# Loading q and k of two heads with one transfer, and taking the second batch's first unit by float32 rows

## Chip, core and metric

The kernel runs on one core of a Trainium2 chip. The metric is the device time of one execution in microseconds, the median of several runs. The engines are PE (TensorE, matmuls), ACT (ScalarE), DVE (VectorE), POOL (GpSimd) and SP (SyncE, which issues all transfers here).

## What is computed

Causal attention with a decay on 4 batches x 8 heads of 576 positions (head dimension 64), and then two feed-forward layers on the 2304 rows that come out of it:

```python
scores = scale * np.matmul(q, k.transpose(0, 1, 3, 2))
log_f = np.log(np.clip(f, 0.0001, 1.0))
cum = np.cumsum(log_f, axis=-1)
scores = np.where(causal, -1000000000.0, scores + cum[..., :, None] - cum[..., None, :])
attn = np.exp(scores - max);  attn = attn / (sum + 1e-09);  x = attn @ v
h = x @ w_in;   y = np.maximum(0.01 * h, h) @ w_out                 # 512 -> 2048 -> 512
g = y @ w_gate; out = (g * sigmoid(g) * (y @ w_val)) @ w_out2       # 512 -> 1536 -> 512
```

All results are float32.

## The kernel before

The program is recorded as a list of operations and put in order by a planner (`Plan`), which knows what each operation reads and writes, estimates durations, and writes out one fixed order for each of the five engines. Each engine, and SP's queue of transfers too, then works through its own order; a transfer on SP whose data isn't ready holds up all that stand behind it. In the first microseconds the planner fills pauses of PE with matmuls that nobody uses.

Attention goes by units: unit (b, u) is batch b, queries 0 to 319 (u = 0, three tiles of queries a head) or 320 to 575 (u = 1, two tiles). Unit (0,0) has a path of its own; the other seven go through `attention`. While a unit's attention runs, PE does the first feed-forward layers (`moe_h`, then `moe_y`) of the unit before; the weights of the second feed-forward layers are loaded, converted and written back in the same time (`place`, from unit (1,1) on). After unit (3,1), at about 500 us, only feed-forward work is left.

For each head `prep_head` loads q and k and `exps` makes the scores, by one of two ways:

- In batch 0, "float32 rows": a tile of 66 rows, 64 of q and k and two that carry the cumulative sums (`rd`), and one plain float32 matmul for each part of a query tile.
- In batches 1 to 3: the host stores q and k twice below each other, so that one transfer of 128 rows (640 columns for u = 0, 832 for u = 1) puts the same 64 rows on both halves of the partitions. ACT casts all 128 rows to a reduced float32 (tile `ta`) and casts the q part to `tb`; DVE subtracts what the cast lost, q into the upper half of `ta` and k into the lower half of `tb`. Four rows of cumulative sums go to `tb` by a transfer of their own. A score part is then two matmuls, one from `tb` (68 rows) and one from `ta` (128 rows). The loads go to two buffers (`xf_ring`), a head each.

The scores go through DVE (mask, maximum), ACT (exponential), and ACT and DVE (probabilities as two float16 parts). A DMA transpose turns them; when both heads of a pair are there, `pv` multiplies them with v on PE, one group of 24 (u = 0) or 30 (u = 1) matmuls with 64 columns of weights, which alternate between the two heads.

Buffers: the g buffers of the feed-forward layer (`g_ring`) are separate for u = 0 and u = 1, 20,480 and 16,384 bytes a partition. The latter's bytes are used under the name `early` until the end of unit (0,1), among others for three more tiles of 66 rows (`xf1_ring`).

Of the kernel before, what the change touches and what calls it, by code (L numbers as in the profile page):

```python
# [9 lines left out]
F32 = mybir.dt.float32  # L10
F32R = mybir.dt.float32r
F16 = mybir.dt.float16
# [9 lines left out]
P = 128  # L22
# [425 lines left out]
def body(ctx, tc, qk, v, f, w_in, w_out, w_gate, w_val, w_out2, out):  # L448
# [38 lines left out]
    gvd = tc.dram_tile([2 * NB2, P, NC * FB2], F32, name="gate_val_dram")  # L487
    cd = tc.dram_tile([R, 4, W], F32, name="cum_dram")
    rd = tc.dram_tile([H, 2, KEYS[1] + UNITS[1][1]], F32, name="rows_dram")


    pool = ctx.enter_context(tc.tile_pool(name="sb", bufs=1))
# [14 lines left out]
    wo_f = wo_t.t.rearrange("p (a d) -> p a d", d=DM)  # L507
    wo = wo_t.t.bitcast(F16).rearrange("p (a l d) -> p a l d", l=2, d=DM)
    PER = [512 // u[1] for u in UNITS]
    g_ring = [Ring([x.rearrange("p (l i q) -> p l i q", l=2, i=n) for x in a_g.cut(2 * n * u[1], F16, NF // n).bufs])  # L510
              for n, u in zip(PER, UNITS)]
    xs_buf = [a_m.cut(NC * 2 * u[1], F16).rearrange("p (c l q) -> p c l q", c=NC, l=2) for u in UNITS]
    n = a_m.at
    gf_ring = [None, None]
# [20 lines left out]
    vv_ring = Ring([x.rearrange("p (c j l d) -> p c j l d", j=2, l=2, d=D) for x in a_a.cut(NK * 4 * D, F16, 5).bufs])  # L535


    early = a_g.t[:, (a_g.at - NF * 2 * UNITS[1][1] * 2) // 4:]
    dg_ring = Ring([early[:, (i + 1) * P:(i + 2) * P] for i in range(3)])
    vf0 = [early[:, 4 * P + i * NK * P:4 * P + (i + 1) * NK * P].rearrange("p (c d) -> p c d", d=P) for i in range(NHP)]  # L540
    n = 4 * P
# [83 lines left out]
    def decay():  # L625
        n0 = UNITS[0][1]
        scr = wo_t.t[:R, :]
        fr, cum, one = (scr[:, i * S:(i + 1) * S] for i in range(3))
        nc.vector.memset(one[:, :S - n0], -8.0)
        one = one[:, S - n0:]  # L630
        nc.urgent = True
        nc.sync.dma_start(fr, f)
        nc.vector.memset(one, 1.0)
        nc.vector.tensor_scalar(out=fr, in0=fr, scalar1=1e-4, scalar2=1.0, op0=ALU.max, op1=ALU.min)
        nc.scalar.activation(out=fr, in_=fr, func=AF.Ln)

        nc.scalar.activation(out=sm(1, "e", 1)[:R, :], in_=fr[:, :1], func=AF.Exp)

        nc.vector.memset(rows0[:, :n0], 8.0)
        nc.vector.memset(rows0[:, 2 * n0:], -8.0)  # L640
        c0 = rows0[:, n0:2 * n0]
        nc.vector.tensor_tensor_scan(out=c0, data0=one, data1=fr[:, :n0], initial=0.0, op0=ALU.mult, op1=ALU.add)

        lib = sm(1, "lib", 1)
        nc.gpsimd.memset(lib, 0.0)
        nc.gpsimd.partition_all_reduce(lib, lib, P, ABSMAX)
        nc.gpsimd.memset(mask, 0.0)
        nc.urgent = False
        scan = next(o for o in reversed(nc.ops) if o.eng == "DVE")

        nc.filler = (banks[-1], mask[:, :P], mask[:, :4 * P])
        nc.gpsimd.affine_select(out=mask[:, 4 * P:], in_=mask[:, 4 * P:], pattern=[[-1, P + hw]],
                                compare_op=ALU.is_ge, fill=NEG, base=0, channel_multiplier=1)
        csf = scr[:, 3 * S:3 * S + 4 * W].rearrange("r (a s) -> r a s", a=4)
        cs = csf.bitcast(F32R)

        for x in ph_ring.bufs:
            for i in (3, 8):
                nc.gpsimd.memset(x.rearrange("p (n k) -> p n k", k=P)[:, i::9, hw:], 0.0)
        nc.behind = scan  # L660
        for u, (q0, nq, _) in enumerate(UNITS):
            col, _, qc, kc = COLS[u]
            for a, c, n in ((0, kc, KEYS[u]), (2, qc, nq)):
                x = csf[:, a:a + 2, col + c:col + c + n]
                nc.scalar.copy(out=x, in_=one[:, :1].unsqueeze(2).to_broadcast(x.shape))
        nc.behind = None
        nc.scalar.copy(out=cum[:, :n0], in_=c0)
        nc.vector.tensor_tensor_scan(out=cum[:, n0:], data0=one[:, :S - n0], data1=fr[:, n0:],
                                     initial=c0[:, n0 - 1:n0], op0=ALU.mult, op1=ALU.add)
        nc.vector.memset(fr, 8.0)  # L670
        for u, (q0, nq, _) in enumerate(UNITS):
            col, wd, qc, kc = COLS[u]
            n = KEYS[u]
            ks = slice(col + kc, col + kc + n)
            qs = slice(col + qc, col + qc + nq)
            nc.vector.tensor_scalar(out=cs[:, 2, ks], in0=cum[:, :n], scalar1=-8.0, scalar2=None, op0=ALU.mult)
            nc.vector.scalar_tensor_tensor(out=cs[:, 3, ks], in0=cum[:, :n], scalar=-8.0, in1=csf[:, 2, ks],
                                           op0=ALU.mult, op1=ALU.subtract)
            nc.scalar.activation(out=cs[:, 0, qs], in_=cum[:, q0:q0 + nq], func=AF.Copy, scale=8.0)
            nc.scalar.activation(out=cs[:, 1, qs], in_=csf[:, 3, col + kc + q0:col + kc + n], func=AF.Copy, scale=-1.0)  # L680
        nc.sync.dma_start(cd, csf)
        nc.sync.dma_start(rd[:, 0, :S], fr[:H, :])
        nc.sync.dma_start(rd[:, 0, S:], cum[:H, n0:])
        nc.sync.dma_start(rd[:, 1, :], scr[:H, S:3 * S - n0])
# [4 lines left out]
    def prep_v(b, hps):  # L689
# [19 lines left out]
        if hp == NHP - 1:  # L709
# [5 lines left out]
            nc.vector.tensor_scalar(out=sc, in0=iv, scalar1=sx, scalar2=1.0 / PSCALE, op0=ALU.mult, op1=ALU.mult)  # L715
            vsc[b] = (sc, ix, sx)

    class Head:
        pass

    def prep_head(b, u, h):
        o = Head()
        o.b, o.u, o.tp, o.sums = b, u, [], sm(3, "sums", 4)
        nq, nk = UNITS[u][1], KEYS[u]
        col, o.wd, qc, kc = COLS[u]
        o.q, o.k = slice(qc, qc + nq), slice(kc, kc + nk)
        if b == 0:
            o.xf = xf1_ring.next()
            nc.sync.dma_start(o.xf[:D, :o.wd], qk[b, h, :D, col:col + o.wd])
            nc.sync.dma_start(o.xf[D:D + 2, :o.wd], rd[h])  # L730
            return o
        xf = xf_ring.next()
        nc.sync.dma_start(xf[:, :o.wd], qk[b, h, :, col:col + o.wd])
        o.tb = tb_ring.next()
        nc.sync.dma_start(o.tb[D:D + 4, :o.wd].bitcast(F32), cd[b * H + h, :, col:col + o.wd])
        o.ta = ta_ring.next()
        taf = o.ta.bitcast(F32)
        nc.scalar.copy(out=o.ta[:, :o.wd], in_=xf[:, :o.wd])
        nc.scalar.copy(out=o.tb[:D, o.q], in_=taf[:D, o.q])
        nc.vector.tensor_tensor(out=o.ta[D:, o.q], in0=xf[D:, o.q], in1=taf[D:, o.q], op=ALU.subtract)  # L740
        nc.vector.tensor_tensor(out=o.tb[:D, o.k], in0=xf[:D, o.k], in1=taf[:D, o.k], op=ALU.subtract)
        return o

    def exp_of(tp, parts, ms, mx, total):
# [12 lines left out]
    def exps(o, n):  # L757
# [10 lines left out]
        nc.begin()  # L768
        for a, e, w in parts:
            ps = ps_s.next()  # L770
            if o.b == 0:
                nc.tensor.matmul(ps[:, :w], lhsT=o.xf[:D + 2, q:q + P],
                                 rhs=o.xf[:D + 2, o.k.start + a:o.k.start + a + w], start=True, stop=True)
            for l in range(2 if o.b else 0):
                t, k = (o.tb, D + 4) if l == 0 else (o.ta, P)
                nc.tensor.matmul(ps[:, :w], lhsT=t[:k, q:q + P], rhs=t[:k, o.k.start + a:o.k.start + a + w],
                                 start=(l == 0), stop=(l == 1))
# [343 lines left out]

    for arena in (a_a, a_g, a_m, wi_t, wo_t, a_w):
        arena.at = 0
    WB = NB2 * 2
    NW = [WB - 4, 2, 2]
    w2 = [x.rearrange("p (k l d) -> p k l d", k=14, l=2)
          for t, n in zip((a_a, a_g, wi_t), NW) for x in t.cut(14 * 2 * P, F16, n).bufs]
# [6 lines left out]
    c_ring = Ring([x.rearrange("p (m k n) -> p m k n", m=2, k=4) for x in wi_t.cut(8 * UH, F32, 2).bufs])  # L1134
    waste2 = wi_t.cut(UN, BF16, 2)

    us_0 = [x.rearrange("p (l a n) -> p l a n", l=2, a=NA)
            for t, n in ((a_g, 6), (a_a, 1)) for x in t.cut(2 * NA * P, F16, n).bufs]
    sum_t = a_g.cut(NA * P, F32).rearrange("p (a n) -> p a n", a=NA)
# [328 lines left out]
```

## Time and profile before

| | us |
|---|---|
| median of 3 runs | 923.5 (923.33 to 925.16) |
| the profiled execution | 925.66 |
| its span, first to last instruction | 923.9 |
| PE busy | 908.8 (98%) |
| DVE busy | 794.1 (86%) |
| ACT busy | 676.1 (73%) |
| POOL busy | 45.4 (5%) |
| DMA engines, mean busy share | 54.2% |

Busy times are unions of an engine's instructions, and ends of matmuls are modelled, so PE's busy share is not a share of its peak. A plain float32 matmul shows as two records, all others as one. What a matmul costs PE is read from the distance between starts. The kernel has a heavy attention part up to about 500 us, in which all engines and the DMA queues are loaded, and a part of matmuls alone after it.

### The profile page before, as it was taken

How to read it: one execution, taken by the hardware profiler on the slowest of the kernel's cores; microseconds unless marked ns; L12 is line 12 of the kernel's file. 1: busy time of each engine (PE TensorE's matmuls, PEld its weight loads, DVE VectorE, ACT ScalarE, POOL GpSimd, SP SyncE). 2: the span in 40 equal slices, each digit the busy share in tenths (PEclk: the TensorE clock that was granted, in tenths of full speed). 3: DMA queues.
4: the chain of work that ended last, by engine and by line, in shares of the span. 5: the costliest groups of instructions: out<-in, count | busy, mean ns of one | idle time of the engine just before them, and what ended most of it. 6: DMA issues, size and time to landing. Idle time of an engine off the chain costs nothing.

```text
span 923.9 us, 25387 instructions
## 1 busy us (share of the span) xinstructions
PE 908.8 (98%) x10018; PEld 776.7 (84%) x10018; DVE 794.1 (86%) x2078; ACT 676.1 (73%) x1665; POOL 45.4 (5%) x119
## 2 busy tenths in 40 slices
PE   9999999999999999899999999999999999999998
PEld 5666678877688777788778899999999999999997
DVE  7999999988899999799788999986778695968685
ACT  8886689988689887688886878774647474755553
POOL 3410000000000010000000000000000000000000
PEclk9999999999999999999999999999999999999999
DMA  7568985797999999989867452110101000100001
GB/s 229 179 202 217 271 212 115 187 248 172 259 270 259 255 263 229 298 249 254 188 147 191 140 178 96 64 59 20 37 18 31 25 25 25 37 25 2 26 6 42
DMA packets 163431, 132.81 MB, mean 144 GB/s; under 512 B 117432, under 2 KB 130752, under 8 KB 163280
## 3 DMA queue, kind: packets, MB, share of 16 engines
q1 hardware_dynamic: 163312, 131.20, 53.5%
q8 instruction: 78, 1.28, 0.6%
q14 instruction: 41, 0.34, 0.1%
HBM read 79.99 MB, written 22.83 MB: 111 GB/s over the span
## 4 chain that ended last, share of the span: by engine, by line
PE 58%; DVE 7%; DMA 3%; ACT 3%; issue 1%; POOL 0%; SPq 0%; ACTq 0%; DVEq 0%; POOLq 0%
PE bank L415 58%; DVE att_bytes L415 2%; DVE stage L415 1%; DVE wo_bytes L415 1%; ACT att_bytes L415 1%; DMA tb<-out_dram 1%; ACT moe_bytes L415 1%; DMA att_bytes<-att_bytes 1%; DVE smalls L415 1%; DVE wi_bytes L415 1%; DMA att_bytes<-in_qk_dram 1%; DMA gate_val_dram<-wo_bytes 1%; DVE g_bytes L415 1%; DVE tb L415 0%; DVE ta L415 0%
## 5 line engine op out<-in xcount | busy, mean ns | idle before, releaser
L415 PEld LDWEIGHTS <-att_bytes 128*128 128x128 f16 (+1 forms) x4062 | 233.8, 100 | 18.3 <-issue 14.7
L415 PEld LDWEIGHTS <-wi_bytes 128*128 128x128 f16 x2292 | 192.2, 98 | 42.4 <-issue 3.1
L415 PE MATMUL bank<-g_bytes,wo_bytes 128*128 128x256 f16 (+2 forms) x1472 | 209.7, 299 | 0.0
L415 PE MATMUL bank<-moe_bytes,wi_bytes 128*128 128x320 f16 (+1 forms) x1536 | 194.5, 286 | 1.5 <-ACT moe_bytes L415 1.5
L415 ACT ACTIVATE att_bytes<-att_bytes,smalls 128x320 f32<-128x320 f32 (+11 forms) x308 | 173.7, 591 | 30.1 <-DVE smalls L415 25.5
L415 PEld LDWEIGHTS <-wo_bytes 128*128 128x128 f16 x1344 | 128.1, 98 | 33.5 <-issue 1.8
L415 DVE TENSOR_TENSOR wi_bytes<-bank,wi_bytes 128x256 f32<-128x256 f32 x270 | 109.4, 418 | 45.0 <-PE bank L415 43.6
L415 PEld LDWEIGHTS <-g_bytes 128*128 128x128 f16 x1620 | 125.9, 98 | 9.0
L415 ACT ACTIVATE wi_bytes<-wi_bytes,smalls 128x256 f32<-128x256 f32 (+2 forms) x129 | 69.9, 555 | 44.9 <-DVE wi_bytes L415 42.4
L415 PE MATMUL bank<-wi_bytes,att_bytes 128*128 128x128 f16 x1680 | 98.7, 219 | 0.5 <-ACT wi_bytes L415 0.3
L415 DVE SCALAR_TENSOR_TENSOR att_bytes<-att_bytes,smalls 128x576 f16<-128x576 f32 (+5 forms) x148 | 86.8, 614 | 4.1 <-ACT att_bytes L415 3.7
L415 PE MATMUL bank<-stage,att_bytes 128*128 128x128 f16 (+1 forms) x1389 | 86.7, 221 | 0.6 <-DVE wi_bytes L415 0.6
L415 ACT COPY wi_bytes<-bank 128x256 f32<-128x256 f32 x108 | 38.4, 363 | 51.8 <-PE bank L415 47.6
L415 DVE CUSTOM_DVE_ANT_0 att_bytes<-bank,att_bytes 128x320 f32<-128x320 f32 (+5 forms) x160 | 67.7, 441 | 7.2 <-PE bank L415 7.1
L415 POOL PARTITION_ALL_REDUCE smalls<-smalls x54 | 28.2, 523 | 757.1 <-DVE smalls L415 718.3
L415 PE MATMUL bank<-att_bytes 128*64 128x256 f16 (+4 forms) x828 | 55.5, 262 | 5.5 <-DMA att_bytes<-att_bytes 5.2
L415 ACT ACTIVATE wi_bytes<-wo_bytes 128x256 bf16<-128x256 f32 x108 | 44.0, 410 | 19.2 <-DVE wo_bytes L415 19.2
L415 PE MATMUL bank<-wo_bytes,g_bytes 128*128 128x256 f16 x432 | 55.0, 273 | 0.0
L415 DVE TENSOR_TENSOR g_bytes<-moe_bytes,g_bytes 128x320 f16<-128x320 f32 (+1 forms) x80 | 44.6, 564 | 8.2 <-ACT g_bytes L415 7.8
L415 PE MATMUL bank<-tb 68*128 68x256 f32 (+3 forms) x144 | 49.9, 360 | 1.7 <-ACT att_bytes L415 1.1
L415 DVE SCALAR_TENSOR_TENSOR stage<-stage 128x512 int32<-128x512 int32 x68 | 46.5, 684 | 0.2
L415 DVE SCALAR_TENSOR_TENSOR wo_bytes<-wi_bytes,smalls 128x512 f32<-128x512 f32 x54 | 40.1, 743 | 6.3 <-ACT wi_bytes L415 6.3
(123 smaller groups left out, 1380.1 us busy)
## 6 DMA issues: line engine op xcount, KB each, us to landing
stage<-in_moe_w_out_dram SPq DMA_DIRECT2D x28, 512.0 KB
att_bytes<-in_qk_dram SPq DMA_DIRECT2D x24, 416.0 KB
stage<-in_moe_w_in_dram SPq DMA_DIRECT2D x16, 512.0 KB
att_bytes<-in_qk_dram SPq DMA_DIRECT2D x24, 320.0 KB
stage<-in_moe_w_gate_dram SPq DMA_DIRECT2D x12, 512.0 KB
stage<-in_moe_w_val_dram SPq DMA_DIRECT2D x12, 512.0 KB
stage<-gate_val_dram SPq DMA_DIRECT2D x12, 512.0 KB
ta<-y_dram SPq DMA_DIRECT2D x18, 256.0 KB
```

What stands on the lines that cost most here:

```text
L415: fn(*args, **kw)
```

## The change

1. In batches 1 to 3 one transfer of 128 rows serves two heads: it begins at the second copy of the even head and ends with the first copy of the odd one, so that the even head lies on the lower and the odd head on the upper half of the partitions. Each head is then prepared from its own half. The cast to `ta` becomes two, of 64 partitions each: all columns to the lower half, and the k columns (320 or 576) to the upper half, which the 128-row cast covered before.
2. Unit (1,0) goes by float32 rows as batch 0 does, with five tiles in `xf1_ring`; its rows come from a new small DRAM tensor (`rd0`) that is written once.
3. Both units' g buffers begin at the same byte, and `early`, which is now in use until the end of unit (1,0), lies behind them. Two weight tiles of the last part move to the end of the same memory.

```diff
+    rd0 = tc.dram_tile([H, 3 * UNITS[0][1]], F32, name="rows0_dram")
...
+    g_ring = []
+    for n, u in zip(PER, UNITS):
+        a_g.at = 0
+        x = a_g.cut(2 * n * u[1], F16, NF // n).bufs
+        g_ring.append(Ring([y.rearrange("p (l i q) -> p l i q", l=2, i=n) for y in x]))
...
-    early = a_g.t[:, (a_g.at - NF * 2 * UNITS[1][1] * 2) // 4:]
+    early = a_g.t[:, NF * UNITS[0][1]:]
...
+        nc.sync.dma_start(rd0, rows0[H:2 * H, :])
...
-        if b == 0:
+        o.one = b + u == 1
+        if o.one:
             o.xf = xf1_ring.next()
             nc.sync.dma_start(o.xf[:D, :o.wd], qk[b, h, :D, col:col + o.wd])
-            nc.sync.dma_start(o.xf[D:D + 2, :o.wd], rd[h])
+            r = rd0[h]
+            nc.sync.dma_start(o.xf[D:D + 2, :o.wd], rd[h] if u else bass.AP(r.tensor, r.offset, [[nq, 2], [1, o.wd]]))
             return o
-        xf = xf_ring.next()
-        nc.sync.dma_start(xf[:, :o.wd], qk[b, h, :, col:col + o.wd])
+        x = h % 2
+        if x == 0:
+            both[0] = xf_ring.next()
+            a = qk[b, h, D:, col:col + o.wd]
+            nc.sync.dma_start(both[0][:, :o.wd], bass.AP(a.tensor, a.offset, [[a.ap[0][0], P], a.ap[1]]))
+        xf = both[0][x * D:(x + 1) * D]
...
-        nc.scalar.copy(out=o.ta[:, :o.wd], in_=xf[:, :o.wd])
+        nc.scalar.copy(out=o.ta[:D, :o.wd], in_=xf[:, :o.wd])
+        nc.scalar.copy(out=o.ta[D:, o.k], in_=xf[:, o.k])
         nc.scalar.copy(out=o.tb[:D, o.q], in_=taf[:D, o.q])
-        nc.vector.tensor_tensor(out=o.ta[D:, o.q], in0=xf[D:, o.q], in1=taf[D:, o.q], op=ALU.subtract)
-        nc.vector.tensor_tensor(out=o.tb[:D, o.k], in0=xf[:D, o.k], in1=taf[:D, o.k], op=ALU.subtract)
+        nc.vector.tensor_tensor(out=o.ta[D:, o.q], in0=xf[:, o.q], in1=taf[:D, o.q], op=ALU.subtract)
+        nc.vector.tensor_tensor(out=o.tb[:D, o.k], in0=xf[:, o.k], in1=taf[:D, o.k], op=ALU.subtract)
...
-            if o.b == 0:
+            if o.one:
...
+    a_g.at = a_g.size - 2 * 14 * 2 * P * 2
```

The planner makes a new order of everything. In it PE's matmuls that nobody uses go from 44 to 43. At three places it reads as follows. On PE, at the first head of unit (1,0), before (`tb` and `ta` are the prepared tiles, `g_bytes,wo_bytes` is feed-forward work of unit (0,0)):

```order
L415 MATMUL bank_69<-tb_86 128x256
L415 MATMUL bank_69<-ta_84 128x256
L415 MATMUL bank_70<-tb_86 128x256
L415 MATMUL bank_70<-ta_84 128x256
L415 MATMUL bank_73<-g_bytes,wo_bytes 128x320
```

and now (tiles of 66 rows lie in `g_bytes` and `att_bytes`):

```order
L415 MATMUL bank_71<-g_bytes 128x256
L415 MATMUL bank_70<-g_bytes 128x256
L415 MATMUL bank_72<-g_bytes 128x320
L415 MATMUL bank_75<-g_bytes,wo_bytes 128x320
L415 MATMUL bank_76<-g_bytes,wo_bytes 128x320
L415 MATMUL bank_71<-g_bytes 128x256
L415 MATMUL bank_70<-g_bytes 128x256
L415 MATMUL bank_72<-g_bytes 128x320
```

Three matmuls a head take the place of six, and the second head's stand close behind the first's.

On SP, at the end of unit (2,1), from the third last transpose of its probabilities to the last, before (`in_qk_dram` is a q/k load, `tb` a transfer of cumulative sums):

```order
L415 DMA_TRANSPOSE att_bytes<-att_bytes 128x18x128
L415 DMA tb_87<-cum_dram 4x640
L415 DMA att_bytes<-in_v_dram 128x640
L415 DMA_TRANSPOSE att_bytes<-att_bytes 128x18x128
L415 DMA stage<-in_moe_w_out_dram 128x1024
L415 DMA att_bytes<-in_qk_dram 128x640
L415 DMA out_dram<-wi_bytes 128x512
L415 DMA att_bytes<-in_qk_dram 128x640
L415 DMA_TRANSPOSE att_bytes<-att_bytes 128x18x128
```

and now:

```order
L415 DMA_TRANSPOSE att_bytes<-att_bytes 128x18x128
L415 DMA out_dram<-wi_bytes 128x512
L415 DMA tb_87<-cum_dram 4x640
L415 DMA att_bytes<-in_qk_dram 128x640
L415 DMA_TRANSPOSE att_bytes<-att_bytes 128x18x128
L415 DMA tb_88<-cum_dram 4x640
L415 DMA stage<-in_moe_w_out_dram 128x1024
L415 DMA_TRANSPOSE att_bytes<-att_bytes 128x18x128
```

Four transfers stood before the last transpose, two of them q/k loads; now two do, and neither is a q/k load. One stands before the transpose ahead of it.

On ACT, at the first heads of unit (1,1), now (`ta` and `tb` casts of two heads; before, each pair of `ta` casts was one of 128x832):

```order
L415 CAST ta_85<-att_bytes 64x832
L415 CAST ta_85<-att_bytes 64x576
L415 CAST tb_87<-ta_85 64x256
L415 ACTIVATE moe_bytes<-bank_73,smalls 128x320
L415 CAST ta_86<-att_bytes 64x832
L415 CAST ta_86<-att_bytes 64x576
L415 CAST tb_88<-ta_86 64x256
```

Each head has one cast more, right behind the first.

## Rows read from the trace of the kernel before

**Rows 1.** The page's busy times: us, share of the span, instructions.

```profile
PE 908.8 (98%) x10018; PEld 776.7 (84%) x10018; DVE 794.1 (86%) x2078; ACT 676.1 (73%) x1665; POOL 45.4 (5%) x119
```

**Rows 2.** Windows of about units (1,0), (2,0) and (3,0); columns in the first line.

```profile
core 0: us, PE busy (x) PEld busy (x) DVE busy (x) ACT busy (x) POOL busy (x), PEclk, DMA share, GB/s
112.00:185.00 73.00, 71.88 (x644) 60.59 (x641) 69.35 (x208) 67.28 (x167) 3.65 (x12) 1.00 0.76 176
252.00:307.00 55.00, 53.91 (x531) 46.80 (x532) 51.92 (x171) 49.12 (x131) 3.69 (x11) 1.00 0.97 257
376.00:433.00 57.00, 57.00 (x549) 49.54 (x547) 52.64 (x162) 49.02 (x130) 0.30 (x2) 0.97 0.95 260
```

**Rows 3.** PE's waits: who for whom, us in total, times, longest.

```profile
PE bank L415 <- DMA att_bytes<-att_bytes: 5.2, 3, 2.3
...
PE bank L415 <- ACT moe_bytes L415: 1.5, 3, 0.7
PE bank L415 <- ACT att_bytes L415: 1.1, 1, 1.1
```

**Rows 4.** Timeline of PE at 371: start, us, instruction, idle before it.

```profile
371.05 0.39 PE L415 MATMUL bank<-tb 68*128 68x256 f32 x1
...
372.03 0.30 PE L415 MATMUL bank<-att_bytes 128*64 128x256 f16 x1
374.68 0.52 PE L415 MATMUL bank<-att_bytes 128*64 128x256 f16 x6 [2.35 <-DMA att_bytes<-att_bytes]
```

**Rows 5.** Timeline of PE at 96: matmuls of 66 rows in unit (0,1).

```profile
96.02 1.14 PE L415 MATMUL bank<-g_bytes 66*128 66x288 f32 x4
97.00 0.70 PE L415 MATMUL bank<-g_bytes,wo_bytes 128*128 128x320 f32 x2
97.54 0.92 PE L415 MATMUL bank<-g_bytes 66*128 66x448 f32 x2
98.29 0.43 PE L415 MATMUL bank<-g_bytes,wo_bytes 128*128 128x320 f32 x1
```

**Rows 6.** Timeline of PE at its other waits in the attention part.

```profile
110.64 1.56 PE L415 MATMUL bank<-att_bytes 128*64 128x256 f16 x29 [1.26 <-DMA att_bytes<-att_bytes]
...
172.36 0.39 PE L415 MATMUL bank<-tb 68*128 68x320 f32 x1 [1.12 <-ACT att_bytes L415]
...
252.31 1.56 PE L415 MATMUL bank<-att_bytes 128*64 128x256 f16 x29 [1.62 <-DMA att_bytes<-att_bytes]
...
435.75 0.43 PE L415 MATMUL bank<-moe_bytes,wi_bytes 128*128 128x320 f16 x2 [0.71 <-ACT moe_bytes L415]
```

**Rows 7.** Timeline of SP ahead of the longest of these waits.

```profile
365.61 0.53 SPq L415 DMA_DIRECT2D stage<-in_moe_w_out_dram  x1
366.19 0.42 SPq L415 DMA_DIRECT2D att_bytes<-in_qk_dram  x1
366.67 0.42 SPq L415 DMA_DIRECT2D out_dram<-wi_bytes  x1
367.21 0.35 SPq L415 DMA_DIRECT2D att_bytes<-in_qk_dram  x1
367.68 4.80 SPq L415 DMA_TRANSPOSE att_bytes<-att_bytes  x1
```

**Rows 8.** Timeline of DVE there: the last probabilities of the head.

```profile
364.38 1.40 DVE L415 SCALAR_TENSOR_TENSOR att_bytes<-att_bytes,smalls 128x576 f16<-128x576 f32 x2
```

**Rows 9.** ACT's groups by shape: count, busy us, mean ns of one, idle before.

```profile
L415 ACT CAST ta<-att_bytes 128x832 fp32r<-128x832 f32 x24 | 21.1, 878 | 1.3 <-PE bank L415 0.6 <-DMA att_bytes<-in_qk_dram 0.5
L415 ACT CAST g_bytes<-moe_bytes 128x512 f16<-128x512 f32 x32 | 19.5, 617 | 0.4
L415 ACT CAST ta<-att_bytes 128x640 fp32r<-128x640 f32 x24 | 17.2, 717 | 0.7 <-DMA att_bytes<-in_qk_dram 0.7
L415 ACT CAST tb<-ta 64x320 fp32r<-64x320 f32 x24 | 10.8, 452 | 0.1
```

**Rows 10.** DMA issues of the page: q/k loads of batches 1 to 3.

```profile
att_bytes<-in_qk_dram SPq DMA_DIRECT2D x24, 416.0 KB
...
att_bytes<-in_qk_dram SPq DMA_DIRECT2D x24, 320.0 KB
```

More of the change, by code (lines that the diff above doesn't have):

```diff
@@ L509, in body @@
     PER = [512 // u[1] for u in UNITS]
-    g_ring = [Ring([x.rearrange("p (l i q) -> p l i q", l=2, i=n) for x in a_g.cut(2 * n * u[1], F16, NF // n).bufs])
-              for n, u in zip(PER, UNITS)]
+    g_ring = []
[3 more added lines that the diff above has]
+        g_ring.append(Ring([y.rearrange("p (l i q) -> p l i q", l=2, i=n) for y in x]))
     xs_buf = [a_m.cut(NC * 2 * u[1], F16).rearrange("p (c l q) -> p c l q", c=NC, l=2) for u in UNITS]
@@ L716, in prep_v @@
             vsc[b] = (sc, ix, sx)
+    both = [None]
     class Head:
@@ L770, in exps @@
             ps = ps_s.next()
-            if o.b == 0:
+            if o.one:
                 nc.tensor.matmul(ps[:, :w], lhsT=o.xf[:D + 2, q:q + P],
                                  rhs=o.xf[:D + 2, o.k.start + a:o.k.start + a + w], start=True, stop=True)
-            for l in range(2 if o.b else 0):
+            for l in range(0 if o.one else 2):
                 t, k = (o.tb, D + 4) if l == 0 else (o.ta, P)
@@ L1135, in body @@
     waste2 = wi_t.cut(UN, BF16, 2)
+    a_g.at = 0
     us_0 = [x.rearrange("p (l a n) -> p l a n", l=2, a=NA)
```

## Prediction

> **What bounds the kernel now.** I read the table of busy times first, then the windows by attention unit, then what PE waited for, and last the timeline around each wait. PE is busy 908.8 of 923.9 us [rows 1], so the sum is built on PE: work added to PE is added to the time one for one, work taken from another engine counts only where PE stood still for it, and the most that any relief can give back is what PE lost. In the windows of units (1,0), (2,0) and (3,0) PE is busy 71.88 of 73, 53.91 of 55 and 57.00 of 57 us, while DVE, ACT and the DMA queues run close behind (DVE 69.35 of 73, ACT 49.12 of 55, DMA share 0.97) [rows 2]. So PE is the bound, but with engines behind it that have little room.
>
> What PE lost, from its waits [rows 3] and the timelines: 5.2 us in three waits for a transposing transfer of the probabilities, 1.26 us before 110.64, 1.62 us before 252.31 and 2.35 us before 374.68; 1.12 us before 172.36 for ACT, at a score matmul that reads a head's prepared tiles; 0.71 us before 435.75 for ACT [rows 4, 6]. [...]
>
> How such a wait comes about can be read at the longest one. DVE finishes the last probabilities of a head at 364.38 + 1.40 = 365.78 us [rows 8]. SP, which issues all transfers in order, is at that moment issuing a weight load, and then takes a q/k load, a store and a second q/k load before it comes to the transpose at 367.68, 1.9 us late; the transpose holds SP for 4.80 us, and PE starts again at 374.68, 7.0 us after the issue [rows 4, 7]. Two of the four transfers ahead are the kind that the change halves.
>
> **The change part by part. Scores of the second batch's first unit.** Eight heads lose six reduced-precision float32 matmuls each (one from tb, one from ta, for three tiles) and get three plain float32 matmuls. The six take from 371.05 to 372.03, 0.98 us a head [rows 4]. For the plain kind the trace has other widths: two matmuls of 288 columns (four records, two for each) go from 96.02 to 97.00, so 0.49 us each, and one of 448 from 97.54 to 98.29, 0.75 us [rows 5]. That is 1.65 ns a column between them; 256 columns give 0.43 us, 320 give 0.54 us, and a head 0.43 + 0.43 + 0.54 = 1.40 us. PE gains 8 x (1.40 - 0.98) = **+3.4 us**, all on the path, since PE has no room in that window. Bounds: +3.2 to +3.6, by the two slopes.
>
> **Preparation of these eight heads** goes: on ACT a 640-column cast of 0.72 us and a 320-column one of 0.45 us a head [rows 9], 9.4 us in all, and on DVE two subtractions a head. The wait before 172.36 is for ACT at just such a head. It should go, **-1.1 us**; bounds 0 (another wait in its place) and -1.1.
>
> **The extra cast.** In the other five units a head's 128-partition cast becomes two of 64 partitions. A 64-partition cast of 320 columns takes 452 ns, and the 128-partition casts lie on one line by columns alone (617 ns at 512, 717 at 640, 878 at 832) [rows 9], so the half-height casts save nothing and the second is pure addition: 16 heads x 0.45 us and 24 heads x 0.66 us (576 columns, an estimate from 640 less 64 columns) = 23.1 us; less the 9.4 us above, ACT gets 13.7 us more. What covers it is ACT's idle time: 55 - 49.12 = 5.9 us in the unit of rows 2 that begins at 252 and 57 - 49.02 = 8.0 us in the one from 376, against 8 x 0.45 = 3.6 us added in each [rows 2]. It is covered on the average but not at every head, because the cast stands between the load and the scores. On the path: 0 to +3.6 us for each of these two units; I take **+1.0 us** in all, near the lower end, because PE's waits for ACT are short today [rows 3].
>
> **The loads.** Before, batches 1 to 3 load 24 tiles of 416 KB and 24 of 320 KB [rows 10], 17.7 MB. After it are 12 and 8, and eight of 160 KB: 8.8 MB less. SP issues 20 of these fewer, 8 transfers of the cumulative sums fewer, and 9 small ones of the rows more. In time this is worth what PE waits for transposes. In SP's order, as the section on the change shows it for the end of unit (2,1), the transfers between the last two transposes of the unit go from four (two of them q/k) to two (none q/k). At 0.42 and 0.35 us an issue with its gaps [rows 7] that is 1 us earlier to the issue of the transpose, and there are 640 KB less of transfers ahead of it in flight. For the wait before 374.68, at the end of unit (2,1), with its clock, bounds 0 and -4.0 us; I take **-2.5**, because the wait is 2.35 us and the two causes seen there are both removed, but PE's work between the scores and their use has not grown. For the wait before 252.31, at the end of unit (1,1), bounds 0 and -1.6, **-0.5**: the issue there is behind stores too. For the wait before 110.64, bounds +1.3 and -1.3, **0**: it lies in unit (0,1), whose loads do not change, and whose order was made anew. For the 0.71 us before 435.75, bounds 0 and -0.7, **-0.5**: ACT's own waits for q/k loads, 0.5 and 0.7 us in all today [rows 9], become fewer.
>
> A transpose that is issued behind a load is seen to be slow here (7.0 us from its issue to PE's restart, 4.80 of them the issue itself) [rows 4, 7]. [...]
>
> **Buffers.** The g buffers of both units now lie on the same bytes. A unit's first g is written after the previous unit's second layer has read it; both follow each other on PE anyway, so I cost it at nothing. If the planner had counted on an overlap there, it would be a wait of ACT of a quarter of a chunk's reads; no row shows one, and I bound it at 0 to +1 us. The filler matmuls go from 44 to 43 and stand in idle time: nothing. The new row transfers are 5 KB each and are issued ahead: nothing, and 0.4 us of SP each if their head is waited for.
>
> **Sum.** +3.4 - 1.1 + 1.0 - 2.5 - 0.5 + 0 - 0.5 = -0.2 us. Against the profiled execution's own time of 925.66 us (span 923.9 and 1.8 around it) that is 925.5; the median of the runs shown is 923.5, 2.2 us lower, so the forecast is 923.5 - 0.2 = **923.3 us**.
>
> **Rivals.** (1) The relief is complete: every wait of a transpose in units (1,1) and (2,1) and both waits for ACT go, and the casts are covered: 3.4 - 1.1 - 4.0 - 1.6 - 0.7 = -4.0, **919.5 us**, with the first wait as well 918.2. For it: both causes at the longest wait are named in SP's timeline, and 8.8 MB are gone from windows with a DMA share of 0.95 and 0.97 [rows 2, 7]. Against it: PE's own work between a pair's scores and its use of the transposes is no longer than before, and the order of everything is made anew, so waits can come up at other places.
>
> (2) The loads were hidden anyway, and the waits of transposes stay as they are, because the transpose itself takes 4.80 us of SP [rows 7]: 3.4 - 1.1 = +2.3, **925.8 us**. Here the change doesn't do what it says.
>
> (3) On the other side, ACT becomes the bound of the first units of batches 2 and 3. Place: between a pair's load and its first score matmul; price: 3.6 us in each of two units where ACT has 5.9 and 8.0 us left [rows 2], half of which is exposed: +3.6; it decides when a unit's remaining idle time of ACT is broken into waits that it can't fill. With 3.4 - 1.1 that is +5.9, **929.4 us**, if the transposes are no better. [...]
>
> **How the numbers follow.** About 0.2%, 1.85 us, is what a measurement of this kernel can tell from no change, so "same" is 921.65 to 925.35. The forecast, waits partly relieved against the dearer scores: 0.40, from 921.7 to 925.3. Rival 1: 0.33, below 921.6. Rival 2: 0.13 and rival 3: 0.14, both above 925.4. So faster 0.33, same 0.40, slower 0.27. The range leaves out about 1 in 10 on either side, past full relief and past half of rival 3's price: 918.0 to 928.5 us. Both signs hold much of the chance; the forecast's own range is 921.7 to 925.3.
>
> **What would show it.** Score matmuls of 66 rows in the window of the second batch's first unit, 256 columns at 0.43 us and 320 at 0.54; if a head takes 1.0 us, the main cost is wrong. ACT's busy total up by about 14 us from 676.1 [rows 1], DVE's down by some 8. PE's waits for transposes down from 5.2 us to 2 or 3, and the granted clock at 1.00 where it is 0.97. If PE's waits for ACT rise above 5 us, rival 3 is right. It would also be wrong if the new order moves PE's waits into units that I took as unchanged, the second unit of the first batch above all.

## The result and the profile after

| | before | changed |
|---|---|---|
| median, us | 923.41 (922.33 to 925.16) | 936.45 (936.28 to 938.54) |
| the profiled execution, us | 925.66 | 936.4 |
| its span, us | 923.9 | 934.3 |

The ratio is 1.0145 with a 95% interval of 1.0123 to 1.0166: 13.0 us slower, and 8 us above the upper end of the forecast's range. The page of the changed kernel begins with the busy times, in the columns of [rows 1]:

```profile
PE 912.7 (98%) x10013; PEld 780.2 (83%) x10017; DVE 789.7 (85%) x2062; ACT 691.2 (74%) x1689; POOL 43.7 (5%) x119
```

ACT has 15.1 us more, DVE 4.4 less, PE 3.9 more. The span is 10.4 us longer (less than the medians differ, because the profiled execution of before is 2.2 us above its median); 3.9 us of it is busy time of PE, and 6.5 us is time in which PE stood. What it stood for, in the columns of [rows 3]:

```profile
PE bank L415 <- DVE smalls L415: 5.2, 6, 2.6
PE bank L415 <- ACT moe_bytes L415: 3.6, 2, 2.3
PE bank L415 <- ACT stage L415: 2.0, 1, 2.0
PE bank L415 <- ACT ta L415: 2.0, 2, 1.4
...
PE bank L415 <- DMA att_bytes<-att_bytes: 0.5, 1, 0.5
```

The waits for transposes are gone, 5.2 us down to 0.5. In their place PE waits, as the profile puts it down, for DVE (5.7 us in all, 1.4 before) and for ACT (8.7 us, 2.9 before). Where the instruction named had ended well before PE went on, it was another. Two places show how.

**The end of unit (0,1) and the start of unit (1,0).** PE's timeline, then DVE's, then SP's, with start, duration and idle time before:

```profile
123.67 1.57 PE L415 MATMUL bank<-g_bytes 66*128 66x256 f32 x6
125.08 1.24 PE L415 MATMUL bank<-g_bytes,wo_bytes 128*128 128x320 f32 x4
126.16 1.03 PE L415 MATMUL bank<-g_bytes 66*128 66x256 f32 x4
129.75 0.81 PE L415 MATMUL bank<-g_bytes 66*128 66x320 f32 x2 [2.56 <-DVE smalls L415]
```

```profile
125.32 0.17 DVE L415 TENSOR_REDUCE smalls<-smalls 128x1 f32<-128x16 f32 x1
128.46 0.82 DVE L415 TENSOR_REDUCE smalls<-att_bytes 128x1 f32<-128x640 f32 x1 [2.98 <-DMA att_bytes<-in_v_dram]
129.20 0.48 DVE L415 CUSTOM_DVE_ANT_0 att_bytes<-bank,att_bytes 128x320 f32<-128x320 f32 x1
```

```profile
119.73 0.47 SPq L415 DMA_DIRECT2D att_bytes<-in_qk_dram  x1
120.24 0.44 SPq L415 DMA_DIRECT2D att_bytes<-rows_dram  x1
120.79 3.10 SPq L415 DMA_TRANSPOSE att_bytes<-att_bytes  x1
123.98 0.54 SPq L415 DMA_DIRECT2D att_bytes<-in_qk_dram  x1
124.58 0.44 SPq L415 DMA_DIRECT2D att_bytes<-rows_dram  x1
125.11 0.37 SPq L415 DMA_DIRECT2D att_bytes<-in_v_dram  x1
```

Read it from the bottom. A load of v stands on SP behind a transpose that holds SP for 3.10 us and is issued at 125.11. In DVE's order the reduction of v's maximum stands ahead of a score tile, so DVE stands 2.98 us although the scores are there. PE goes on at 129.75, 0.07 us behind the end of DVE's reading of that score tile (129.20 + 0.48 = 129.68); that its next matmul needs the tile's place in PSUM is my inference from these times. Then the clock falls; windows of the changed kernel, columns as in [rows 2]:

```profile
112.00:132.00 20.00, 16.89 (x83) 11.63 (x83) 15.68 (x54) 12.01 (x33) 1.40 (x8) 0.97 0.89 205
132.00:185.00 53.00, 53.00 (x478) 44.58 (x477) 41.08 (x123) 42.31 (x105) 1.07 (x3) 0.95 0.44 104
...
130.00:137.60 7.60, 7.54 (x40) 5.08 (x40) 4.83 (x23) 4.88 (x14) 0.32 (x3) 0.55 0.21 68
```

From 130 to 137.6 the granted clock averages 0.55, and from 131 to 137 it is 0.50. This costs PE 7.6 x (1 - 0.55) = 3.4 us, an estimate from these numbers. After the wait of 2.35 us before 374.68 in the kernel before [rows 2, 4] it was 57 x (1 - 0.97) = 1.7 us by the same estimate, with the clock at 0.51 from 375.9 to 379.31.

**The last heads of unit (3,0).** ACT's timeline, DVE's and PE's at the same time:

```profile
424.56 1.21 ACT L415 CAST ta<-att_bytes 64x640 fp32r<-64x640 f32 x2
...
426.61 0.80 ACT L415 ACTIVATE att_bytes<-att_bytes,smalls 128x256 f16<-128x256 f32 x2
427.31 0.51 ACT L415 ACTIVATE moe_bytes<-bank,smalls 128x320 f16<-128x320 f32 x1
```

```profile
426.59 1.30 DVE L415 SCALAR_TENSOR_TENSOR att_bytes<-att_bytes,smalls 128x320 f16<-128x320 f32 x3
427.81 0.48 DVE L415 CUSTOM_DVE_ANT_0 att_bytes<-bank,att_bytes 128x320 f32<-128x320 f32 x1
```

```profile
428.40 0.39 PE L415 MATMUL bank<-tb 68*128 68x320 f32 x1 [2.34 <-ACT moe_bytes L415]
```

The `x2` in ACT's first row is the pair of casts. The wait is put down to ACT, but the instruction named ends at 427.31 + 0.51 = 427.82. What ends 0.11 us before PE goes on is DVE's reading of a score tile from its PSUM bank (427.81 + 0.48 = 428.29). In DVE's order three subtractions of probabilities stand ahead of it. The second cast is not what makes this wait: the changed kernel with one cast a head (e7, below) has it at the same place, again 0.11 us behind DVE's reading there (422.30 + 0.48 = 422.78):

```profile
422.89 0.39 PE L415 MATMUL bank<-tb 68*128 68x320 f32 x1 [2.14 <-ACT ta L415]
```

The wait of 0.71 us before 435.75 in [rows 6] is gone.

### The profile page after: what moved, and what is told of

Read it like the earlier page. It is cut to its first block, busy times and chain, and to the rows that moved or that the text cites. A ratio compares the mean times of both kernels' runs of the same rounds, so it can differ in the third digit from the quotient of the medians.

```text
span 934.3 us, 25301 instructions
## 1 busy us (share of the span) xinstructions
PE 912.7 (98%) x10013; PEld 780.2 (83%) x10017; DVE 789.7 (85%) x2062; ACT 691.2 (74%) x1689; POOL 43.7 (5%) x119
## 4 chain that ended last, share of the span: by engine, by line
PE 53%; ACT 1%; DVE 1%; issue 0%; DVEq 0%; ACTq 0%
PE bank L415 53%; DVE wi_bytes L415 0%; ACT L415 0%; ACT att_bytes L415 0%; ACT stage L415 0%; ACT ta L415 0%; ACT wi_bytes L415 0%; DVE stage L415 0%; ACT moe_bytes L415 0%; DVE moe_bytes L415 0%; ACT tb L415 0%; DVE smalls L415 0%; DVEq L415 0%; ACTq L415 0%
## 5 line engine op out<-in xcount | busy, mean ns | idle before, releaser
L415 ACT ACTIVATE att_bytes<-att_bytes,smalls 128x448 f16<-128x448 f32 (+11 forms) x308 | 173.4, 589 | 35.9 <-DVE smalls L415 27.5
L415 DVE CUSTOM_DVE_ANT_0 att_bytes<-bank,att_bytes 128x320 f32<-128x320 f32 (+6 forms) x160 | 68.2, 443 | 10.8 <-PE bank L415 10.6
L415 PE MATMUL bank<-att_bytes 128*64 128x256 f16 (+5 forms) x846 | 63.1, 271 | 1.0 <-DMA att_bytes<-att_bytes 0.5
L415 ACT CAST ta<-att_bytes 64x832 fp32r<-64x832 f32 (+1 forms) x80 | 56.0, 700 | 3.0 <-PE bank L415 1.6
L415 PE MATMUL bank<-tb 68*128 68x288 f32 (+3 forms) x120 | 42.5, 364 | 8.9 <-DVE smalls L415 2.4
```

The lines of the kernel that those rows point to most:

```text
L415: fn(*args, **kw)
```

## The experiments

Medians are of each run's own comparison; the kernel before took 923.25 to 924.02 us beside them. "Made anew" means that the planner ordered the edited program; in the other kernels the recorded order is kept, and only what an entry of it does is changed.

**1. Which part costs.** The first kernel has the pair loads and both casts, without the float32 rows and with the buffers of before; the second has the rows and the buffers, with a load a head and one cast. Both orders made anew.

```diff
# e1_pairs_only: before, and
+        if x == 0:
+            both[0] = xf_ring.next()
+            nc.sync.dma_start(both[0][:, :o.wd], bass.AP(a.tensor, a.offset, [[a.ap[0][0], P], a.ap[1]]))
-        nc.scalar.copy(out=o.ta[:, :o.wd], in_=xf[:, :o.wd])
+        nc.scalar.copy(out=o.ta[:D, :o.wd], in_=xf[:, :o.wd])
+        nc.scalar.copy(out=o.ta[D:, o.k], in_=xf[:, o.k])
# e2_rows_only: the changed kernel with these lines of before
```

> The change without its second half: one load for two heads and two casts a head in batches 1 to 3, unit (1,0) prepared as before, g buffers as before; the planner orders it anew. Theory A (the second cast puts ACT on PE's path): 929 to 932 us, with waits of PE for ACT of 6 us or more. Theory B (most of the loss is one bad place in the changed kernel's order, DVE standing before a late load of v at 127 us while PE's clock falls): 921 to 925 us. Theory C (the plain float32 scores of unit (1,0) are the loss): 920 to 923 us.

> The other half alone: unit (1,0) by float32 rows and the moved buffers, but a load of 128 rows and one cast a head in the other units. Theory A: 926 to 928 us, the 3.4 us of the scores alone. Theory B: 926 to 928 if the bad place doesn't come up, 931 to 934 if it does. Theory C: 930 us or more without any bad place.

Pairs alone: 929.9 us, ratio 1.0059 (1.0036 to 1.0082). Rows alone: 930.56, ratio 1.0065 (1.0039 to 1.009). The parts lose 6.6 and 7.3 us, and together 13.0: within the intervals they add up. Pairs alone has theory A's time without its sign: PE's waits put down to ACT are 3.0 us, those for DVE 6.4. Rows alone lies between the ranges of its theories. It has the stand at 127 us too (2.89 us), so the pair loads are not its cause.

**2. Other draws.** The planner rates its candidate orders with random delays; both kernels were ordered with other ones.

```diff
-            r = random.Random(k)
+            r = random.Random(k + 100)
```

> The kernel before with other random draws in the planner's trials, so the same operations in another order. Theory A: within 2 us of 923.4. Theory B: orders of one program differ by 3 us or more, in either direction.

> The changed kernel with other random draws in the planner's trials. Theory A: 934 to 938 us, waits of PE for ACT as large as in the changed kernel. Theory B: 927 to 931 us, without the wait at 127 us.

The kernel before took 923.7 us in an order that differs on every engine (on SP at 93 of 423 transfers, by the trace), ratio 0.9994 (0.9979 to 1.001). The changed kernel got the same order again and took 936.13 us, a repeat. So the old time isn't the luck of one order. Whether the new one is, these two don't tell.

**3. One step at a time, order kept.** Before with a second, redundant cast at all 48 heads; before without the odd heads' loads; the changed kernel with one cast of 128 partitions; the changed kernel without the late load of v.

```diff
# e5_before_extra_casts
+        op.calls.append((copy, (), dict(out=o.ta[D:, o.k], in_=xf[D:, o.k])))
# e6_before_half_loads (but for two heads)
+        if h % 2: nc.ops[-1].calls.clear()
# e7_after_one_cast
-        nc.scalar.copy(out=o.ta[:D, :o.wd], in_=xf[:, :o.wd])
-        nc.scalar.copy(out=o.ta[D:, o.k], in_=xf[:, o.k])
+        nc.scalar.copy(out=o.ta[:, :o.wd], in_=both[0][:, :o.wd])
# e8_after_no_v_load
+                if (b, hp) == (1, 2): nc.ops[-1].calls.clear()
```

> The kernel before in its own order, with the second cast (64 partitions, 320 or 576 columns) done once more behind the first at all 48 heads; nothing else moves. ACT gets 24 x 0.45 + 24 x 0.66 = 26.7 us. Theory A: +5 to +9 us. Theory B: at most +2 us.

> The kernel before in its own order, with the q/k load of every odd head of batches 1 to 3 left out (but for the first pair of units (1,0) and (1,1)); those heads take what the buffer holds. It measures what half the q/k transfers are worth by themselves. If transposes wait because of q/k loads: -3 to -8 us, PE's waits for transposes down from 5.2 to under 2 us. If they were hidden: within 1 us.

> The changed kernel in its own order, with one cast of 128 partitions in the place of the two of 64; the upper half of a tile then holds k of the pair's odd head, the scores of even heads' upper part are wrong. ACT loses 23 us. Theory A: -5 to -9 us. Theory B: 0 to -2 us.

> The changed kernel in its own order, with one load of v left out (batch 1, third pair of heads, the one that DVE waits for at 125 to 128 us); the pair takes the v that the buffer holds. Theory B: -5 to -7 us, 2.6 us of PE's wait and 3.4 us of the clock. Theory A: 0 to -2 us.

Casts added, 27.2 us more of ACT: 940.77 us, +17.0. Loads left out: 919.04, -4.7. One cast in the changed kernel: 931.44, -5.0. Load of v left out: 931.92, -4.5, just under the range of theory B. The stand at 127 us is gone in the last one (timeline of PE):

```profile
126.28 1.57 PE L415 MATMUL bank<-g_bytes 66*128 66x256 f32 x6
127.76 1.36 PE L415 MATMUL bank<-att_bytes 66*128 66x256 f32 x5
```

The load of v is thus shown to be the cause at this place. The clock is at 1.00 from 130 to 137.6 us there, but at 0.97 from 252 to 307 and from 376 to 433 us, where the changed kernel's profile has 1.00, so the end shows a little less than the place gives back.

Not all of the 5.0 us of e7 belong to the casts. The first of the 40 heads with casts comes at 183.7 us in the changed kernel, and in e7 the clock has fallen for a shorter time long before that:

```profile
130.00:137.60 7.60, 7.54 (x51) 5.69 (x51) 6.20 (x25) 6.29 (x18) 0.32 (x3) 0.78 0.23 80
```

With 0.78 in the place of 0.55 this is 7.6 x 0.23 = 1.7 us, so by these two profiles some 3.3 us are left for the casts.

The price of the casts in e5 was far above what I had expected, and left a contradiction: 17 us for 27 us of ACT here, while pairs with both casts lose only 6.6.

**4. Without ACT's second cast, orders made anew.** The pair loads with the second cast on POOL, and with one cast of 128 partitions.

```diff
# e9_pairs_on_gpsimd: e1, and
-        nc.scalar.copy(out=o.ta[D:, o.k], in_=xf[:, o.k])
+        nc.gpsimd.tensor_copy(out=o.ta[D:, o.k], in_=xf[:, o.k])
# e10_pairs_one_cast: e1, and one cast as in e7; e15: the same with other draws
```

> The pair loads alone, without the float32 rows, with the second cast (the k columns to the upper half) on POOL in the place of ACT; order made anew. The pair loads with both casts on ACT gave 929.9 us. Theory A: the loss of the pair loads is ACT's time, and the halved loads by themselves give back 4.7 us; then this one lies at 918 to 922, PE's waits for transposes under 2 us, and PE waits for ACT no more than before. Rival B: it is not ACT but one more step between a pair's load and its scores, whichever engine takes it; then POOL's cast, slower than ACT's 0.45 to 0.66 us, leaves it at 927 to 933 us and PE or DVE is seen to wait for POOL's tiles.

> The pair loads alone, order made anew, with one cast of 128 partitions a head and no second one: the upper half of a head's tile then holds the other head's k where its own belongs, so the second-order part of the scores is not the reference's; sizes and counts of all other work are those of the kernel before. Theory A (the second cast on ACT is the loss): 917 to 921 us, ACT's busy time back to about 677, 9 to 12 us less than with both casts. Rival B (the new order, or the halved loads' other rhythm, is the loss): 926 to 931 us, with DVE or DMA waits of PE as long as in the run with both casts.

> The pair loads alone with one cast of 128 partitions, as in the run that gave 926.9 us (the upper half again holds the other head's k), but ordered by other random draws of the planner. Theory A (each new order carries its own few us of waits, of either size): anything from 920 to 931 us, at other places than before, more than 2 us away from 926.9. Rival B (something in the pair loads makes every order slower than 919): 925 to 929 us with waits for DVE and transposes at the same units as in that run.

928.07 us on POOL, 926.92 with one cast, and 927.91 in the other order. My theory fell: without the second cast the pair loads are still 3 to 4 us slower than the kernel before, in both orders and by waits at several of the same places (near 121, 135, 165, 411 and 421 us), not 4.7 us faster. Against 929.9 with both casts, the second cast costs 2 to 3 us by the medians where the planner orders around it, and 1.0 to 1.6 us by the ratios; the intervals overlap, so this price is not clear of the noise.

**5. Buffers alone, and half of the score matmuls.** The change's buffers with unit (1,0) as before, order made anew; and the changed kernel, order kept, with the float32 score matmuls of unit (1,0) over half of their columns.

```diff
# e11_buffers_only: e2, and
-        o.one = b + u == 1
+        o.one = b == 0
# e12_after_half_width_scores: in unit (1,0)
-   out ps[:, :w],       rhs o.xf[:D + 2, k0 + a:k0 + a + w]
+   out ps[:, :w // 2],  rhs o.xf[:D + 2, k0 + a:k0 + a + w // 2]
```

> The change's buffers alone (both units' g buffers at the same byte, the early tiles behind them, the rows' DRAM tensor), while the second batch's first unit and all loads and casts stay as before; order made anew. With the float32 rows on these buffers it took 930.6 us. Theory A: the buffers cost nothing, 922.5 to 925, and the 7.3 us of that run belong to the rows of the second batch's first unit and the order that they bring. Rival B: half or more of the 7.3 us is the overlap of the g buffers, a wait of ACT's writes of g for PE's reads at each change of unit; then 927 to 931 us and PE waits for ACT at g tiles at changes of unit.

> The changed kernel in its own order, with the float32 score matmuls of the second batch's first unit over half of their columns (128, 128 and 160 in the place of 256, 256 and 320); the other half of those scores is left out. Theory A: PE is the bound through that unit, and half of 8 x 1.40 us is saved one for one: 5.6 us less than 936.4, 930.5 to 931.5 us; the stand behind the late load of v at about 127 us stays as long as it is. Rival B: DVE or SP is the bound of that unit once its scores come so late, and PE only waits longer: 934 to 936.5 us, with more of PE's waits for DVE in the window from 112 to 190 us.

Buffers alone: 925.27 us, ratio 1.0019 (0.9997 to 1.0041), between nothing and half of what the rows cost. Half scores: 935.06 us, 1.4 less by the medians, not 5.6. At the stand nothing is gained, as PE's timeline shows:

```profile
125.79 0.61 PE L415 MATMUL bank<-g_bytes 66*128 66x128 f32 x4
130.16 0.90 PE L415 MATMUL bank<-g_bytes 66*128 66x160 f32 x2 [3.77 <-DVE smalls L415]
```

PE gets to the same place earlier, and stands 3.77 us in the place of 2.56 for the same load of v. Behind the stand the time does come back. The first score matmul of unit (1,1), in the changed kernel and then with half scores, and PE's next wait in the latter:

```profile
188.50 0.44 PE L415 MATMUL bank<-tb 68*128 68x448 f32 x1
```

```profile
184.63 0.45 PE L415 MATMUL bank<-tb 68*128 68x448 f32 x1
...
188.01 1.00 PE L415 MATMUL bank<-att_bytes 128*64 128x64 f16 x23 [2.05 <-DMA att_bytes<-att_bytes]
```

Here 3.9 of the 5.6 us are gained. Some of it goes at this wait for a transpose, and some where the clock averages 0.97 from 376 to 433 us in the place of 1.00. The latter is not the edit's doing: the profile of e4, the changed kernel once more, has 0.97 there too (over the whole run 0.995, in the changed kernel's profile 0.996).

**6. The real pair loads in the order of before.** Each pair load stands at the place of the even head's load. One cast (e16); both casts on ACT (e13); the second on POOL (e14); one cast, and a spare one of the same length behind the cast to `tb`, which no score waits for (e17). The last kernel is e6 with the loads in the pair's form.

```diff
+            pair[0] = xf_ring.bufs[h // 2 % 2]   # even heads; odd heads' loads go
# e16:  ta[:, :o.wd] from pair[0][:, :o.wd]
# e13:  + ta[D:, o.k] from the head's half, ACT      e14: the same, POOL
# e17:  e16, and + tb[96:P, o.k] from pair[0][96:P, o.k], ACT
# e18:  e6, with a load's source as in the pair loads
```

> The order of before on every engine, with the real pair loads (each in the place of the even head's load, the odd head's load gone) and the second cast directly behind the first on ACT. Compare 919.0 us with the odd loads left out and 940.8 with a second cast at all 48 heads and the old loads. Theory A (ACT's time is the loss where the order does not know of it): 919.0 plus about 0.64 us for each us of cast, 26.7 us of them: 933 to 937 us. Rival B (the new order is the loss, the second cast costs about the 3 us by which the replanned kernels with one and with two casts differ): 921 to 924 us.

> The order of before on PE, DVE and SP, with the real pair loads and the second cast on POOL at the place where ACT's cast stands; ACT keeps a cast of 64 partitions, as long as its old one of 128. Theory A (new order and ACT's second cast are the loss, the pair loads themselves a gain): 918.5 to 921 us, below both kernels, PE's waits for transposes near 1 us. Rival B (a head's tile is ready later by POOL's longer cast, and DVE and POOL slow each other): 924 to 930 us, DVE busy up by 5 us or more and PE waiting for POOL or DVE at ta tiles.

> The order of before on every engine, the real pair loads in the place of the even heads' loads, and one cast of 128 partitions from the pair's tile in the place of the old one (the upper half then holds the other head's k where its own belongs; all sizes as before). Theory A (the pair loads are a gain and the second cast is what costs): 918 to 920.5 us, as with the odd loads left out. Rival B (the pair load itself loses the gain): 923 to 927 us, with DMA waits of PE for q/k or transposes of 3 us or more.

> The kernel of the run before this one, with a cast of the k columns more a head on ACT, 32 partitions wide and as long as the second cast, behind the head's cast to tb and into rows of tb that no matmul reads: 26 us more of ACT, but nothing that this head's scores wait for. With the second cast on the chain, directly behind the first, the same order took 942.8 us. Theory A (ACT's time as such is the price: what stands behind the cast in ACT's order comes later): 932 to 943 us. Rival B (the price is the step on the chain from load to scores): within 4 us of the run with one cast.

> The kernel in the order of before with the odd heads' loads of q and k left out (919.0 us; the odd heads are computed from what lies in their buffer), with one thing changed: each remaining load begins at the even head's second copy and ends with the odd head's first, as the pair loads do. Theory A (the form of the transfer costs nothing): 918 to 920.5 us, waits as in that run. Rival B (the transfer that spans two heads is itself slower, as its longer issue at one place, 0.50 us in the place of 0.33, suggests): 922.5 to 925 us, as with the real pair loads.

| | us | ratio to before |
|---|---|---|
| e16, one cast | 923.85 | 0.9992 (0.9978 to 1.0006) |
| e13, both on ACT | 942.78 | 1.0194 (1.0164 to 1.0223) |
| e14, second on POOL | 931.0 | 1.0075 (1.0047 to 1.0103) |
| e17, spare cast | 940.0 | 1.0176 (1.0161 to 1.0191) |
| e18, odd loads left out, pair form | 919.19 | 0.9952 (0.9935 to 0.9969) |

The spare cast settles why a cast is dear. PE's waits with one cast (first) and with the spare one (second):

```profile
PE bank L415 <- DMA tb<-cum_dram: 2.4, 2, 1.9
...
PE bank L415 <- ACT moe_bytes L415: 1.5, 2, 1.1
...
PE bank L415 <- ACT att_bytes L415: 1.1, 1, 1.1
PE bank L415 <- DVE smalls L415: 1.0, 2, 0.7
PE bank L415 <- DMA att_bytes<-att_bytes: 0.7, 2, 0.5
```

```profile
PE bank L415 <- DVE smalls L415: 5.7, 7, 1.7
PE bank L415 <- ACT moe_bytes L415: 4.4, 6, 1.4
PE bank L415 <- ACT att_bytes L415: 4.2, 3, 2.0
```

and their busy times:

```profile
PE 906.9 (98%) x10014; PEld 776.1 (84%) x10018; DVE 795.9 (86%) x2078; ACT 676.6 (73%) x1665; POOL 45.2 (5%) x119
```

```profile
PE 912.8 (97%) x10014; PEld 777.5 (83%) x10018; DVE 798.1 (85%) x2078; ACT 704.7 (75%) x1713; POOL 45.0 (5%) x119
```

28.1 us more of ACT, on which no score depends, make the kernel 16.1 us longer, nearly as much as the 18.9 us of the cast on the chain (942.78 - 923.85, with 29.6 us more of ACT). So it is ACT's time as such. The waits put down to ACT, and to DVE, which itself works on what ACT delivers (in e16 it waits 5.7 us for ACT's `att_bytes`), grow from 3.6 to 14.3 us in these rows. PE's own busy time grows by 5.9 us over the same matmuls; about 3.1 us of this is the lower clock (0.98 from 307 to 376 us and 0.97 from 376 to 433, 1.00 without the cast), the rest is not explained. e13 and e14 came out dearer than either of their theories.

The same runs show the worth of the relief. With the real pair loads and nothing else (e16) the waits for transposes are down to 0.7 us, further than forecast, but the time is that of the kernel before: a wait of 1.9 us for a head's cumulative sums is new, and others are longer. All waits of PE sum to 10.9 us, against 11.6 before and 8.4 in e6. This is rival B's time, but not by the waits that it named. The 4.7 us of e6 are no measure of the pair loads: with the same transfers (e18) they stay, with heads that read the pair's tile (e16) they go. In e6 and e18 the odd heads wait for no load at all. That this is the difference is not shown: in e16's profile, too, no cast and no subtraction waits for a q/k load. What takes the gain stays open.

## Why the prediction was wrong

The sum was -0.2 us, the result 13.0. By the runs three terms failed: the loads (-3.5, measured +3 to +4 in the new orders), order and buffers (put at nothing without a price, 4.5 at one place), and the cast (+1.0, measured 1 to 3, by a wrong reason).

**The extra cast, +1.0 us: wrong reason.** I wrote that it is covered by ACT's idle time, 5.9 and 8.0 us in two units, and compared sums of idle time with sums of work. ACT works through its fixed order, and its idle time there lies in pieces: from 252 to 307 us nine waits for DVE and PE, 5.5 us in all and none above 1.4; from 376 to 433 twelve, 7.1 us in all and none above 1.0. A cast added to that order makes the whole longer even where no score waits for it: 16.1 us for e17's spare ones. Measured for the second cast: 18.9 us for 48 heads in an order that doesn't allow for the casts, 1 to 3 us where the planner makes its order with them, some 3.3 us for 40 heads in the changed kernel's own order (e7, without the clock's part). The length of a cast was right:

```profile
L415 ACT CAST ta<-att_bytes 64x832 fp32r<-64x832 f32 x24 | 21.1, 880 | 1.5 <-PE bank L415 1.2
L415 ACT CAST ta<-att_bytes 64x576 fp32r<-64x576 f32 x24 | 16.1, 670 | 0.6
```

670 ns where I had estimated 660, and 880 on 64 partitions where [rows 9] has 878 on 128. My reason, that PE's waits for ACT were short, describes an order in which the casts are not there.

**The loads, -3.5 us: right wait, wrong worth.** The waits of [rows 6] for transposes did go, more fully than forecast, and where loads are merely left out (e6) the gain comes too. With the real pair loads other waits stand in their place, which the sum had not allowed for. They give -0.2 us in the old order (between -2.0 and +0.6 by the interval), and lose 3 to 4 us in either new one. PE's waits for transposes are down from 5.2 us to 0.7 in e16; the time shows none of the gain. The bound of -4.0 us for the wait before 374.68 counts 1.7 us of clock beside the 2.35 us of the wait. No run shows this term by itself: e6's 4.7 us, at a mean clock of 1.0 over the run where the kernel before has 0.998, hold waits and clock together, and in e16 the clock is at 1.00 from 376 to 433 us, where it was 0.97, and the kernel takes the time of before.

**Order and buffers: nothing, 0 to +1.** The text named the danger, waits in units taken as unchanged, and gave it no price. It holds the largest single wait: the late load of v at the end of unit (0,1), with the clock behind it, 4.5 us by e8. It comes with the float32 rows. The buffers alone may cost up to 3.8 us, 1.6 by the medians.

**The scores, +3.4 us, all on the path.** The size is right: three matmuls a head take 125.08 - 123.67 = 1.41 us, forecast 1.40. The path is right for the most part: by e12, 3.9 of 5.6 us taken away are there at the start of unit (1,1). The rest is lost at the stand for v, where DVE and its load end last, and at the end of the kernel only 1.4 us are left.

**The preparation that goes, -1.1 us.** The wait before 172.36 is gone, and no other stands near it, but I misread it: the ACT instruction named ends at 172.04, and what ends 0.10 us before the matmul is DVE's reading of a score tile (171.78 to 172.26), not a head's preparation. At 435.75, where I took -0.5, no wait is left; one of 2.34 us stands ahead of it, at 428.40 (shown above).

**The rivals.** Rival 3, ACT as the bound, came nearest, and its mark was met: waits for ACT above 5 us (8.7 by the profile, 6.4 without the wait at 428.40, which is DVE's). But its price, 929.4 us, was too low, and it lacked the new order's own wait. Of the 13.9 us that the two parts lose, the runs account for about 3.5 by the order around the pair loads, 2.5 by the second cast, 4.5 by the load of v, and 1.6 by buffers. Each of these is good to some 2 us, so that the rest, some 2 us, is within the noise; the dearer scores must lie in it.

No kernel here with pair loads and each head's own k in its tile is below the kernel before; the nearest, on POOL, is at 928.07 us.

## What to carry to other kernels

Where PE is at 98% and every engine works through a fixed order, price an added instruction by the time it takes of its engine, not by the idle time that the engine has: here 0.57 to 0.64 us of the whole for each us of ACT, on or off the chain, until the order is made with it. Price the relief of a wait by the next wait behind it, and check that by leaving the load out *and* by the real replacement, since the two differed by some 4.6 us here. Before a wait is put down to an engine, see that the instruction named ended just before it. When the planner makes a new order, look first for a load queued behind a transpose whose consumer stands ahead of other work in an engine's order.

## What had not been expected of the hardware

The prediction had no casts on POOL; e14's expectation names this as a rival. With 48 casts on POOL (e14, first) some of DVE's operations are longer than in the same order without (e16, second), these the most, 233 ns on the mean against 168:

```profile
L415 DVE TENSOR_SCALAR smalls<-smalls 128x2 f32<-128x2 f32 x32 | 7.5, 233 | 1.6 <-ACT att_bytes L415 0.7
```

```profile
L415 DVE TENSOR_SCALAR smalls<-smalls 128x2 f32<-128x2 f32 x32 | 5.4, 168 | 1.6 <-ACT att_bytes L415 0.6
```

and DVE's busy time is 804.4 us, 8.5 more over the same 2078 instructions, while POOL gets 34.0 us more. The rival's words are that DVE and POOL slow each other; POOL's own reductions are not longer in e14, 516 ns on the mean against 522 in e16. Why DVE's operations are longer is not shown. Moving work to an idle POOL was not free: 7.1 us in this order. How much of that is DVE's longer operations, and how much the later tiles (POOL's casts take 637 and 794 ns), is not shown.
